# The loads of an attention and feed-forward kernel: Q and K of two batches in 512-byte pieces, V rows loaded once, no transfers issued by ScalarE, small first token blocks

## The chip, the cores and the metric

The kernel runs on one core of a Trainium2 chip. A core has TensorE (PE, with its weight loads listed apart as PEld), VectorE (DVE), ScalarE (ACT), GpSimd (POOL) and SyncE (SP); 16 DMA engines move data between the device's main memory and the core's on-chip memory SBUF. Transfers are issued by SP, ACT or POOL; a row named SPq, ACTq or POOLq in the profile is the time that the issuing queue spent on it. PE writes its results to PSUM, from where ACT or DVE copy them. The metric is the time of one execution on the device, in microseconds.

## The reference

Windowed attention over 8 batches of 8 heads, 576 positions and 64 channels, then a feed-forward layer on the 4,608 tokens.

```python
def _attn_ref(q, k, v):
    ...
    scores = scale * np.matmul(q, k.transpose(0, 1, 3, 2))
    mask = np.abs(pos[:, None] - pos[None, :]) <= window
    scores = np.where(mask, scores, -1000000000.0)
    ...
    attn = attn / (np.sum(attn, axis=-1, keepdims=True) + 1e-09)
    return np.matmul(attn, v)

def _moe_ref(x, w_in, w_out, s, b):
    h = x @ w_in
    r = np.maximum(h, 0.0)
    g = s * (r * r) + b
    return (g @ w_out)
```

The window is 32 positions to each side, the model width 512 (8 heads of 64), the hidden width 2,048. Q, K, V, the weights and the output are float32.

## The kernel before

**Attention.** Each batch is cut into three thirds of 192 positions, each third into two *units* of four heads (two pairs). A unit (`unit`, L420) is a chain: PE scores into the PSUM tile SC (`sc`, L435), ACT exponential (L442), DVE product with the band mask (L445), PE row sums and values (`ss` and `av`, both L458), ACT logarithm and exponential, which give the reciprocal (L465, L468), DVE product into XT (L472). The keys of a third are its 192 positions and 32 on each side, taken as two overlapping blocks of 128. There is one SC, and the scores of a unit wait in PE's order for the `av` of the unit before.

**Getting Q, K and V there.** Per batch, Q and K come in five blocks of up to 128 rows each, V in six blocks of 128 rows, two for each third, that overlap (704 rows in place of 576). A row of one head is 64 float32 numbers, so the pieces of these transfers are 256 bytes (`load`, L289). A block lands in a float32 staging tile (STG, one slot for each block), DVE casts it to bf16 (`cast`, L379), and Q and K are then transposed so that channels lie on partitions: in batch 0 by PE (`transpose_pe`, L402) with a copy out of PSUM by ACT for Q (L407) and by DVE for K (L410); in all later batches by a DMA transpose that SP issues (`transpose_dma`, L387). QT, KT and VB have two slots, for alternate batches; STG and the bf16 tiles NAT have one, so a batch's loads follow the casts of the batch before. Batch 0 is loaded by SP and ACT in turn (`plan0`, L322 to L327), later batches by SP for Q and K and by POOL for V. In batch 1, Q and K wait for the sixth weight piece and V for the seventh.

**Feed-forward.** The tokens are cut into blocks (TBLK, L225): 384, 128, then eight of 512. For each block, stage one (`s1`, `w`, L525) gives 16 tiles of 128 hidden channels with four matmuls each; ACT takes the positive part (L531) and DVE squares it (L534). Stage two (`s2`, `o`, L543) multiplies each 128 tokens with `w_out` in 16 matmuls, DVE scales and adds a constant row (L555), SP stores it (L558). The constant row comes from a column sum of `w_out` (L564, L567). Stage one of a block needs all units whose tokens lie in it. The weights are eight pieces that POOL loads with a cast to bf16 (L310, L314); each waits for the one two before it, the first two for pieces of K and V of batch 0.

**Order.** Every step is a task with an assumed cost, a key and its dependences. `_Graph.plan` (L84) is a planner that takes, again and again, the task that can start first by these costs, the smaller key at a tie; the order is then fixed for each engine, and each engine runs its tasks in that order, waiting on semaphores. The key of a unit is below all stage steps, so a unit goes first once it is ready; `after` holds a unit back until a given step of stage one has started (L505).

## Time and profile before

| | us |
|---|---|
| median of 3 runs (lowest, highest) | 372.65 (370.83, 373.82) |
| the profiled execution | 375.49 |
| its span, first to last instruction | 373.8 |
| PE busy | 319.2 |
| ACT busy | 206.4 |
| DVE busy | 193.2 |
| POOL busy | 44.7 |

The profile shows one execution. The busy time of PE is not PE at its peak, because matmuls are pipelined and their ends are modelled. DMA moved 52.71 MB, of 127,869 packets 116,672 under 512 bytes; 38.80 MB were read from main memory and 9.44 MB written to it. Main readings below are the slices of the span, the table by stretch, the waits, and rows of the timeline in order of time; a bracket at the end of a row tells for how long the engine had been idle and what ended it.

### The profile page before, as it was taken

The numbers are of one execution on the slowest core, as the hardware profiler recorded it, in microseconds if no ns is written. First come the engines' busy times: TensorE is split into PE (matmuls) and PEld (weight loads), VectorE is DVE, ScalarE is ACT, GpSimd is POOL, SyncE is SP. The second block draws the span as 40 slices with busy tenths as digits, with TensorE's granted clock in tenths as the row PEclk, the third lists the DMA queues.
The fourth block names the chain that finished last, engine by engine and source line by source line (L and its number), as shares of the span: only waits on it lengthen the run. The fifth ranks groups of instructions, "written<-read, shape, count | busy, mean of one in ns | idle before, by whom it ended". The sixth has DMA issues, their size and how long they took to land.

```text
span 373.8 us, 6108 instructions
## 1 busy us (share of the span) xinstructions
PE 319.2 (85%) x2385; PEld 155.5 (42%) x2424; DVE 193.2 (52%) x439; ACT 206.4 (55%) x310; POOL 44.7 (12%) x62
## 2 busy tenths in 40 slices
PE   1277985935499999988898899989999999999996
PEld 0144543523244444443444344434444444444442
DVE  4363525745556775676585586454444453333321
ACT  1266732255368678767677576657676764434300
POOL 3012241342221210121111000000000000000000
PEclk9999998975599999999999999999999999999999
DMA  8979999999999999999899798863000001001012
GB/s 164 208 110 187 190 225 206 202 190 213 230 221 147 180 200 231 186 198 193 188 172 213 132 174 174 189 141 89 28 31 31 28 30 56 28 30 56 28 58 84
DMA packets 127869, 52.71 MB, mean 141 GB/s; under 512 B 116672, under 2 KB 120768, under 8 KB 127840
## 3 DMA queue, kind: packets, MB, share of 16 engines
q1 hardware_dynamic: 113648, 36.32, 54.2%
q0 software_dynamic: 7424, 14.29, 19.8%
q10 hardware_dynamic: 6768, 1.70, 2.7%
q8 instruction: 19, 0.31, 0.4%
q14 instruction: 10, 0.08, 0.1%
HBM read 38.80 MB, written 9.44 MB: 129 GB/s over the span
## 4 chain that ended last, share of the span: by engine, by line
PE 54%; DMA 19%; SPq 9%; DVE 7%; ACTq 3%; ACT 3%; issue 2%; DVEq 0%
PE o L543 25%; PE w L525 22%; DMA stgq<-in_q_dram 12%; DMA stgk<-in_k_dram 7%; SPq L300 6%; ACTq L300 3%; SPq L387 3%; PE ss L458 3%; PE sc L435 2%; DVE ex L445 2%; PE av L458 2%; ACT ex L442 1%; DVE xt L472 1%; DVE vb L379 1%; DVE gt L534 1%
## 5 line engine op out<-in xcount | busy, mean ns | idle before, releaser
L525 PE MATMUL w<-xt,win 128*128 128x512 bf16 (+2 forms) x624 | 146.4, 367 | 5.5 <-DVE xt L472 4.2
L543 PE MATMUL o<-wout,gt 128*128 128x512 bf16 x554 | 141.5, 382 | 6.0 <-DVE cvec L567 4.0
L525 PEld LDWEIGHTS w<-xt,win 128*128 128x128 bf16 x640 | 59.4, 100 | 71.8 <-issue 5.1
L543 PEld LDWEIGHTS o<-wout,gt 128*128 128x128 bf16 x576 | 53.2, 98 | 65.5 <-DVE cvec L567 4.2
L442 ACT ACTIVATE ex<-sc,zero 128x1024 bf16<-128x1024 f32 x48 | 53.2, 1109 | 12.1 <-PE sc L435 12.1
L445 DVE TENSOR_TENSOR ex<-ex,mask 128x1024 bf16<-128x1024 bf16 x48 | 33.0, 688 | 33.2 <-ACT ex L442 32.7
L300 POOL DMA_DIRECT2D stgv<-in_v_dram x42 | 35.7, 853 | 120.5 <-DVE vb L379 111.5
L465 ACT ACTIVATE lns<-ss,zero 128x384 f32<-128x384 f32 x48 | 27.7, 578 | 27.6 <-PE ss L458 27.5
L531 ACT ACTIVATE r_29<-w,zero 128x512 bf16<-128x512 f32 (+2 forms) x40 | 25.7, 643 | 30.7 <-PE w L525 30.6
L458 PE MATMUL ss<-ex,ones 128*64 128x128 bf16 x384 | 22.1, 244 | 20.5 <-DVE ex L445 20.1
L531 ACT ACTIVATE r_28<-w,zero 128x512 bf16<-128x512 f32 (+2 forms) x40 | 25.7, 642 | 23.1 <-PE w L525 22.6
L531 ACT ACTIVATE r_31<-w,zero 128x512 bf16<-128x512 f32 (+2 forms) x40 | 25.7, 644 | 23.0 <-PE w L525 22.0
L531 ACT ACTIVATE r_30<-w,zero 128x512 bf16<-128x512 f32 (+2 forms) x40 | 25.7, 643 | 19.2 <-PE w L525 18.8
L555 DVE SCALAR_TENSOR_TENSOR outs<-o,sb_36,cvec 128x512 f32<-128x512 f32 x36 | 26.8, 746 | 13.2 <-PE o L543 12.8
L472 DVE TENSOR_TENSOR xt<-av,rec 128x384 bf16<-128x384 f32 x48 | 26.5, 552 | 11.5 <-ACT rec L468 11.2
L379 DVE CAST natq<-stgq 128x512 bf16<-128x512 f32 (+1 forms) x40 | 17.2, 432 | 25.3 <-DMA stgq<-in_q_dram 25.0
L458 PEld LDWEIGHTS ss<-ex,ones 128*64 128x64 bf16 x384 | 13.6, 119 | 39.6 <-DVE ex L445 26.7
L468 ACT ACTIVATE rec<-lns,zero 128x384 f32<-128x384 f32 x48 | 29.3, 610 | 0.8
L435 PE MATMUL sc<-qt,kt 64*128 64x128 bf16 x384 | 21.2, 237 | 9.0 <-ACT qt L407 5.3
L534 DVE TENSOR_TENSOR gt<-r_29 128x512 bf16<-128x512 bf16 (+2 forms) x40 | 15.8, 396 | 22.7 <-ACT r_29 L531 22.7
L534 DVE TENSOR_TENSOR gt<-r_31 128x512 bf16<-128x512 bf16 (+2 forms) x40 | 15.8, 396 | 22.3 <-ACT r_31 L531 22.0
L534 DVE TENSOR_TENSOR gt<-r_30 128x512 bf16<-128x512 bf16 (+2 forms) x40 | 15.8, 394 | 18.6 <-ACT r_30 L531 18.6
(43 smaller groups left out, 134.4 us busy)
## 6 DMA issues: line engine op xcount, KB each, us to landing
out_dram<-outs SPq DMA_DIRECT2D x36, 256.0 KB, 2.3
stgq<-in_q_dram SPq DMA_DIRECT2D x31, 256.0 KB, 5.8
stgk<-in_k_dram SPq DMA_DIRECT2D x29, 256.0 KB, 6.0
stgv<-in_v_dram POOLq DMA_DIRECT2D x28, 256.0 KB, 5.7
stgv<-in_v_dram POOLq DMA_DIRECT2D x14, 192.0 KB, 5.9
win<-in_moe_w_in_dram POOLq DMA_DIRECT2D x4, 512.0 KB, 6.4
wout<-in_moe_w_out_dram POOLq DMA_DIRECT2D x4, 512.0 KB, 5.8
stgq<-in_q_dram SPq DMA_DIRECT2D x8, 128.0 KB, 5.9
```

Of the source, the lines that this page charges most:

```text
L300: lambda e: e.dma_start(STG[n][p0:p1, blk, :].rearrange("p (h d) -> p h d", h=H), src_of[n][b, :, s0:s0 + ns, :].rearrange("h s d -> s h d ...
L435: fns.append(lambda e, u=u, pr=pr, a=a, hh=hh: e.matmul(SC[:, hh, 256 * u + 128 * a:256 * u + 128 * a + 128], lhsT=KT[slot][64 * hh:64 * h ...
L442: add("act", lambda e: e.activation(EX[e_][:, :, :], SC[:, :, :], AF.Exp, bias=ZERO_F[:, :], scale=0.125), 1130.0, reads=["SC", "ZERO"], w ...
L445: add("dve", lambda e: e.tensor_tensor(EX[e_][:, :, :], EX[e_][:, :, :], MASK[:, :, :], ALU.mult), 700.0, reads=[("E", e_), "MASK"], write ...
L458: fns.append(lambda e, u=u, a=a, hh=hh, dst=dst, lhs=lhs: e.matmul(dst[64 * hh:64 * hh + 64, 192 * u + 64 * a:192 * u + 64 * a + 128], lhs ...
L465: add("act", lambda e: e.activation(LNS[e_][:, :], SS[:, 0:384], AF.Ln, bias=ZERO_F[:, :], scale=1.0), 600.0, reads=["SS", "ZERO"], writes ...
L468: add("act", lambda e: e.activation(REC[e_][:, :], LNS[e_][:, :], AF.Exp, bias=ZERO_F[:, :], scale=-1.0), 600.0, reads=[("LNS", e_), "ZERO ...
L472: add("dve", lambda e: e.tensor_tensor(XT[:, prs[0]:prs[1] + 1, x0:x0 + 192], AV[:, 0:384].rearrange("p (u c) -> p u c", u=2), REC[e_][:, ...
L525: add("pe", [lambda e, kc=kc: e.matmul(W[wb][:, 0:nt], lhsT=WIN_BF[:, kc, ft * 128:(ft + 1) * 128], rhs=XT[:, kc, t0:t0 + nt], start=(kc = ...
L531: add("act", lambda e: e.activation(R1[rb][:, 0:nt], W[wb][:, 0:nt], AF.Relu, bias=ZERO_F[:, :], scale=1.0), 280 + 0.82 * nt, reads=[("W", ...
L534: add("dve", lambda e: e.tensor_tensor(GT[gs][:, ft, 0:nt], R1[rb][:, 0:nt], R1[rb][:, 0:nt], ALU.mult), 160 + 0.53 * nt, reads=[("R1", rb ...
L543: add("pe", [lambda e, fc=fc: e.matmul(O[ob][:, :], lhsT=GT[gs][:, fc, sub * 128:sub * 128 + 128], rhs=WOUT_BF[:, fc, :], start=(fc == 0), ...
```

## The change

Q and K of batches 0 and 1 (`NPE = 2`) are loaded by thirds: `load2` takes two neighbouring rows of a head as one piece of 512 bytes, so a partition holds rows 2p and 2p + 1 of the third, 96 partitions in all. `cast2` casts such a third and puts even and odd rows apart, `transpose_pe` transposes it in eight PE transposes of 96 rows, and one copy, which interleaves even and odd columns again, brings it to QT or KT: in batch 0 by ACT for Q and DVE for K, over the four banks of W and O; in batch 1 by DVE for both, over the two halves of SC. Batches 2 to 7 keep their blocks and the DMA transposes.

V is loaded by POOL in every batch, each row once (pieces of 96, 128, 64, 128, 64, 96 rows); the 64 rows that two blocks share are copied by a second cast, `cast_v`. ACT issues no transfers. The weights no longer wait for anything and stand in POOL's queue behind V of batch 0; Q and K of batch 1 still wait for the sixth piece. The token blocks are 384, 128, 256, 384, six of 512, and 384. In batch 0 the scores of a unit no longer wait for the `av` of the unit before, and units of batches 0 and 1 are held back by nothing else; from batch 2 on, `rel` counts back from the block that needs a unit (PACE, LEAD). The logarithm is written to the tile of the reciprocal. Dependences on QT and KT are kept by 64 columns (`grans`) instead of 128.

```diff
-sizes = [384, 128]
+sizes = [384, 128, 256, 384]
...
-    STG = {n: sb((128, NBLK, DM), F32, "stg" + n) for n in "qk"}
-    STG["v"] = sb((128, 2 * NT3, DM), F32, "stgv")
-    NAT = {n: sb((128, NBLK, DM), BF16, "nat" + n) for n in "qk"}
+    STG = {n: sb((128, 6, DM), F32, "stg" + n) for n in "qkv"}
+    NAT = {n: sb((128, 6, DM), BF16, "nat" + n) for n in "qk"}
...
-    LNS = [sb((128, 384), F32, "lns") for _ in range(2)]
...
+    PACE, LEAD = 2.6, 7
+    NPE = 2
+    EVAC0 = {"q": "act", "k": "dve"}
...
-    def load(b, n, blk, stream="sp", waits=()):
+    VROWS = [(WIN, 128), (0, 128), (64, 128), (0, 128), (64, 128), (0, 96)]
+    def key_of(b, part):
+        return 16 * (b - 1) + part
+    def load(b, n, blk, waits=()):
         if n == "v":
-            k0 = 192 * (blk // 2) - WIN + 128 * (blk % 2)
-            p0, p1 = max(0, -k0), min(128, S - k0)
-            s0 = k0 + p0
+            p0, p1 = VROWS[blk]
...
-            stream,
+            "pool" if n == "v" else "sp",
...
-            1070.0 if stream != "pool" else 1900.0, writes=[("STG", n, blk)],
-            key=16 * (b - 2), waits=waits,
-            dma=({"sp": "l", "act": "a", "pool": "w"}[stream], ns * 9.3))
+            900.0 if n == "v" else 1070.0, writes=[("STG", n, blk)], key=key_of(b, -16), waits=waits,
+            dma=("v" if n == "v" else "l", ns * 9.3))
+    def load2(b, n, t, waits=()):
+        return add(
+            "sp",
+            lambda e: e.dma_start(
+                STG[n][0:96, 2 * t:2 * t + 2, :].rearrange("p a (h x) -> p (a h) x", h=NPAIR),
+                src_of[n][b, :, 192 * t:192 * t + 192, :].rearrange("h (p r) d -> p h (r d)", r=2),
+            ),
+            1000.0, writes=[("STG", n, 2 * t), ("STG", n, 2 * t + 1)], key=key_of(b, -16), waits=waits,
+            dma=("l", 768 * 27 / 16.0))
...
-        return add("pool", fn, 1000.0, writes=[("W" + which, i)], waits=waits, key=-50,
+        return add("pool", fn, 1000.0, writes=[("W" + which, i)], waits=waits, key=-30,
                    dma=("w", 2550.0))
...
-    first = {}
-    plan0 = [("q", 0, "sp"), ("k", 0, "act"), ("q", 1, "sp"), ("k", 1, "act"), ("v", 0, "sp"),
...
-             ("v", 5, "sp")]
-    for n, blk, stream in plan0:
-        first[n, blk] = load(0, n, blk, stream)
+    for n, t in (("q", 0), ("k", 0), ("k", 1), ("q", 1), ("k", 2), ("q", 2)):
+        load2(0, n, t)
+    for blk in range(6):
+        load(0, "v", blk)
...
-    wts = []
-    for i in range(8):
-        wait = [first["k", 3]] if i == 0 else [first["v", 5]] if i == 1 else [wts[i - 2]]
-        wts.append(load_weights("in" if i < 4 else "out", i % 4, waits=wait))
+    wts = [load_weights("in" if i < 4 else "out", i % 4) for i in range(8)]
...
+    def cast_v(b, blk):
+        slot = b % 2
+        key = key_of(b, -8)
+        pad = [("STGPAD", blk)] if blk in (0, 2 * NT3 - 1) else []
+        p0 = 64 if blk in (2, 4) else 0
+        add("dve", lambda e: e.tensor_copy(VB[slot][p0:128, blk, :], STG["v"][p0:128, blk, :]),
+            380.0, reads=[("STG", "v", blk)] + pad, writes=[("VB", slot, blk)], key=key)
+        if blk in (2, 4):
+            add("dve", lambda e: e.tensor_copy(VB[slot][0:64, blk, :], STG["v"][64:128, blk - 1, :]),
+                380.0, reads=[("STG", "v", blk - 1)], writes=[("VB", slot, blk)], key=key,
+                accum=False)
...
-        add("sp", lambda e: e.dma_start(dst[:, :, s0:s0 + ns], NAT[n][0:ns, blk, :],
-                                        transpose=True),
-            1300.0, reads=[("NAT", n, blk)], writes=[(n + "T", slot, blk)],
-            dma=("t", 700.0), key=16 * (b - 1) - 6)
+        c0 = s0 if n == "q" else s0 + WIN
+        add("sp", lambda e: e.dma_start(dst[:, :, c0:c0 + ns], NAT[n][0:ns, blk, :], transpose=True),
+            1250.0, reads=[("NAT", n, blk)], writes=grans(n, slot, s0, s0 + ns),
+            dma=("t", 1000.0), key=key_of(b, -6))
+    def cast2(b, n, t):
+        add("dve", lambda e: e.tensor_copy(
+            NAT[n][0:96, 2 * t:2 * t + 2, :].rearrange("p r (h d) -> p r h d", h=H),
+            STG[n][0:96, 2 * t:2 * t + 2, :].rearrange("p a (g r d) -> p r (a g) d", r=2, d=D)),
+            700.0, reads=[("STG", n, 2 * t), ("STG", n, 2 * t + 1)],
+            writes=[("NAT", n, 2 * t), ("NAT", n, 2 * t + 1)], key=key_of(b, -8))
...
+    def transpose_pe(b, n, t, banks, evac):
+        slot = b % 2
...
-        res = banks[tcount[b] % len(banks)]
-        tcount[b] += 1
...
-        add("pe", [lambda e, pr=pr: e.transpose(view[:, pr, 0:ns],
-                                                NAT[n][0:ns, blk, pr * 128:(pr + 1) * 128],
-                                                IDENT[0:ns, 0:ns]) for pr in range(NPAIR)],
...
+        res, bank = banks[tcount["n"] % len(banks)]
+        tcount["n"] += 1
+        view = bank.bitcast(BF16)[:, 0:768].rearrange("p (r g c) -> p r g c", r=2, g=NPAIR)
+        c0 = 192 * t + (0 if n == "q" else WIN)
+        to = dst[:, :, c0:c0 + 192].rearrange("p g (x r) -> p r g x", r=2)
+        key = key_of(b, -6)
+        add("pe", [lambda e, r=r, pr=pr: e.transpose(view[:, r, pr, :],
+                                                     NAT[n][0:96, 2 * t + r, pr * 128:(pr + 1) * 128],
+                                                     IDENT[0:96, 0:96])
+                   for r in range(2) for pr in range(NPAIR)],
+            450, reads=[("NAT", n, 2 * t), ("NAT", n, 2 * t + 1), "IDENT"], writes=[res], key=key)
+        fn = (lambda e: e.copy(to, view)) if evac == "act" else (lambda e: e.tensor_copy(to, view))
+        add(evac, fn, 900, reads=[res], writes=grans(n, slot, 192 * t, 192 * t + 192), key=key)
...
-        add("pe", fns, 310.0, reads=qk_res, writes=["SC"], key=key + 0.5,
-            after=after + ([("av", n - 1)] if n > 1 else []), name=("qk", n))
+        add("pe", fns, 310.0, reads=qk_res, writes=[("SC", 0), ("SC", 1)], key=key + (0.5 if b > 0 else 0),
+            after=after + ([("av", n - 1)] if b > 0 else []), name=("qk", n))
...
-        add("act", lambda e: e.activation(LNS[e_][:, :], SS[:, 0:384], AF.Ln,
+        add("act", lambda e: e.activation(REC[e_][:, :], SS[:, 0:384], AF.Ln,
                                           bias=ZERO_F[:, :], scale=1.0),
...
+    rel, nxt = {}, 1e9
+    for b in range(B - 1, 0, -1):
+        for t in range(NT3 - 1, -1, -1):
+            for g2 in (1, 0):
+                nxt = min(nxt - PACE, 16 * first_block(b * S + 192 * t) - LEAD)
+                rel[b, t, g2] = nxt
     for b in range(B):
-        if b > 0:
+        banks = ([(("W", 0), W[0][:, :]), (("W", 1), W[1][:, :]), (("O", 0), O[0][:, :]),
+                  (("O", 1), O[1][:, :])] if b == 0 else
+                 [(("SC", hh), SC[:, hh, :]) for hh in range(2)])
+        if b < NPE:
+            steps = [("q", 0), ("k", 0), ("k", 1), 0, ("q", 1), ("k", 2), 1, ("q", 2), 2]
+            if b > 0:
+                for x in steps:
+                    if isinstance(x, tuple):
+                        load2(b, *x, waits=[wts[5]] if b == 1 else ())
+                for blk in range(6):
+                    load(b, "v", blk)
+        else:
+            steps = [0, 1, 2]
             for blk in range(NBLK):
                 for n in "qk":
-                    load(b, n, blk, waits=[wts[5]] if b == 1 else ())
-            for blk in range(2 * NT3):
-                load(b, "v", blk, "pool", waits=[wts[6]] if b == 1 else ())
...
-        for n, blk in order:
-            cast(b, n, blk)
...
+                    load(b, n, blk)
+            for blk in range(6):
+                load(b, "v", blk)
...
+            for blk in range(NBLK):
+                for n in "qk":
+                    cast(b, n, blk)
+                    transpose_dma(b, n, blk)
+        for x in steps:
+            if isinstance(x, tuple):
+                cast2(b, *x)
+                transpose_pe(b, *x, banks, EVAC0[x[0]] if b == 0 else "dve")
                 continue
-            if b == 0:
-                transpose_pe(b, n, blk, banks, "act" if b == 0 and n == "q" else "dve")
-            else:
-                transpose_dma(b, n, blk)
-        for t in range(NT3):
+            cast_v(b, 2 * x)
+            cast_v(b, 2 * x + 1)
...
             for g2 in range(2):
...
-                    i = 3 * (b - 1) + t
-                    r = 32 + 6 * (i - 3) - 7 + 3 * g2
-                    r = max(r, 0 if i < 3 else 32)
-                    after = [("s1", r // 16, r % 16)]
-                unit(b, t, g2, after)
+                r = int(rel[b, x, g2]) if b >= NPE else -1
+                unit(b, x, g2, [("s1", r // 16, r % 16)] if r >= 0 else [])
```

54 lines of the change are left out of this document (13 added, 41 removed).

## The prediction

> **What bounds the kernel now.** I read the page's slices first, then the busy time by stretch, then the waits and the timeline of the stretches that are not full. The slices show busy tenths of 40 slices of 9.3 us: PE, its granted clock, and the share and rate of the DMA engines.
>
> ```profile
> PE   1277985935499999988898899989999999999996
> ...
> PEclk9999998975599999999999999999999999999999
> DMA  8979999999999999999899798863000001001012
> ```
>
> DMA is full to about 235 us, PE is full from 100 us on. The table by stretch (start:end, length, then busy time of PE, PEld, DVE, ACT, POOL, then clock, DMA share, GB/s) is cut at the first stage-one matmul (31.88), the first score matmul of batch 1 (75.2), the next stage-one matmul (99.25) and the last transpose (255.15):
>
> ```profile
> 0.00:31.88 31.88, 12.31 (x144) 8.29 (x144) 14.86 (x42) 13.14 (x19) 6.05 (x16) 1.00 1.01 166
> 31.88:75.20 43.32, 37.83 (x245) 20.12 (x250) 20.79 (x58) 18.01 (x38) 13.85 (x17) 0.96 1.18 201
> 75.20:99.25 24.05, 8.97 (x146) 6.46 (x146) 12.76 (x27) 13.26 (x18) 6.45 (x9) 0.58 1.17 210
> 99.25:255.15 155.90, 145.94 (x1171) 68.34 (x1191) 98.73 (x224) 107.19 (x157) 18.37 (x22) 0.99 1.05 183
> 255.15:373.80 118.65, 114.11 (x683) 52.29 (x695) 46.11 (x90) 54.81 (x80) 0.00 (x0) 0.99 0.11 43
> ```
>
> After 99.25 PE works with few gaps to the end. So the end is set by PE's work, and what can be won are PE's losses, nearly all before 99.25. The waits of PE (engine, line, releaser: us in total, times, longest), the first two from the stretch 31.88 to 99.25, the last two from 100 on:
>
> ```profile
> PE ss L458 <- DVE ex L445: 11.8, 6, 2.0
> PE w L525 <- DVE xt L472: 4.2, 2, 3.3
> ```
>
> ```profile
> PE sc L435 <- DMA kt<-natk: 3.7, 2, 2.0
> PE ss L458 <- DVE ex L445: 3.6, 3, 1.6
> ```
>
> The start (timeline rows: start, length, engine, line):
>
> ```profile
> 4.10 0.29 POOL L353 TENSOR_SCALAR_AFFINE_SELECT mask<-mask 128x128 bf16<-128x128 bf16 x1
> 4.79 0.43 DVE L379 CAST natq<-stgq 128x512 bf16<-128x512 f32 x1 [1.68 <-DMA stgq<-in_q_dram]
> 12.12 2.38 ACTq L300 DMA_DIRECT2D stgk<-in_k_dram  x1
> 14.54 0.59 ACT L407 COPY qt<-w 128x512 bf16<-128x512 bf16 x1 [12.44 <-issue]
> 15.76 0.61 PE L435 MATMUL sc<-qt,kt 64*128 64x128 bf16 x8 [5.35 <-ACT qt L407]
> 16.40 1.11 ACT L442 ACTIVATE ex<-sc,zero 128x1024 bf16<-128x1024 f32 x1 [0.79 <-PE sc L435]
> 17.55 0.69 DVE L445 TENSOR_TENSOR ex<-ex,mask 128x1024 bf16<-128x1024 bf16 x1 [4.64 <-ACT ex L442]
> 18.97 0.58 ACT L465 ACTIVATE lns<-ss,zero 128x384 f32<-128x384 f32 x1 [0.98 <-PE ss L458]
> 20.48 0.42 DVE L410 COPY kt<-w 128x512 bf16<-128x512 bf16 x1 [1.56 <-PE w L402]
> 20.96 0.60 ACT L468 ACTIVATE rec<-lns,zero 128x384 f32<-128x384 f32 x1
> 21.85 0.55 DVE L472 TENSOR_TENSOR xt<-av,rec 128x384 bf16<-128x384 f32 x1
> 30.37 0.61 PE L435 MATMUL sc<-qt,kt 64*128 64x128 bf16 x8
> 31.88 2.74 PE L525 MATMUL w<-xt,win 128*128 128x384 bf16 x8 [0.91 <-DVE xt L472]
> ```
>
> ACT's copies of Q wait behind its own DMA issues until 14.54, although the first data were cast from 4.79 on. Then the units (one third, two head pairs) follow each other every (30.37 - 15.76) / 4 = 3.65 us, since each score group waits for the unit before it. Stage one starts at 31.88.
>
> The hole in the middle, and below it the price of plain PE work (from the chain of waits: start, length, engine, line, count):
>
> ```profile
> 41.98 0.37 SPq L300 DMA_DIRECT2D stgq<-in_q_dram  x1
> 42.24 0.74 POOL L314 DMA_DIRECT2D wout<-in_moe_w_out_dram  x1 [2.26 <-DMA wout<-in_moe_w_out_dram]
> 59.13 0.43 DVE L379 CAST natq<-stgq 128x512 bf16<-128x512 f32 x1 [6.99 <-DMA stgq<-in_q_dram]
> 62.56 1.31 SPq L387 DMA_TRANSPOSE qt<-natq  x1
> 74.93 1.19 SPq L387 DMA_TRANSPOSE kt<-natk  x1
> 75.20 0.40 PE L435 MATMUL sc<-qt,kt 64*128 64x128 bf16 x8
> 77.53 0.41 PE L458 MATMUL ss<-ex,ones 128*64 128x128 bf16 x8 [1.93 <-DVE ex L445]
> 99.25 1.06 PE L525 MATMUL w<-xt,win 128*128 128x512 bf16 x2 [3.27 <-DVE xt L472]
> ```
>
> ```profile
> 316.67 0.86 PE w L525 x4
> ```
>
> Batch 1 is asked for at 41.98, its ten transposes are issued from 62.56 to 74.93, and its six units then run alone, since the third token block (512 wide) needs all of them. A 512-wide matmul costs 0.86 / 4 = 0.215 us; a unit has three groups of about 0.40 us with some overlap, 1.1 us in all. From 31.88 to 99.25 PE did 64 stage-one equivalents (13.8 us), 64 of stage two (13.8), 16 for the column sum (3.4) and 8 units (8.8): 39.8 us in 67.4. **27.6 us are lost there.**
>
> DMA rates, each for its own window: Q and K alone in 256-byte pieces (8 to 15 us), the POOL queue beside SP's (46 to 59, two rows), weights alone (34 to 41), and the output's 2 KB pieces (368 to the end, 40 slices of GB/s):
>
> ```profile
> DMA packets 5884, 1.48 MB, mean 212 GB/s; under 512 B 5884, under 2 KB 5884, under 8 KB 5884
> ```
>
> ```profile
> q0 software_dynamic: 947, 1.94, 71.9%
> q1 hardware_dynamic: 3548, 0.89, 44.8%
> ```
>
> ```profile
> DMA packets 1309, 1.31 MB, mean 187 GB/s; under 512 B 32, under 2 KB 1309, under 8 KB 1309
> ```
>
> ```profile
> GB/s 0 0 99 381 339 395 410 184 0 0 0 0 0 0 0 0 0 0 0 0 0 0 0 0 0 0 141 381 410 339 395 142 0 0 0 0 0 0 0 0
> ```
>
> **The change part by part.** The sum is made against the profiled execution (375.49 us, 0.8% above the median of the runs shown).
>
> *512-byte pieces.* Not in the trace; between 212 GB/s (256 B) and about 390 (2 KB). I take 300, nearer to the 256-byte row's side by the piece's size. A batch's Q and K (2.36 MB) then take 7.9 us, between 6.1 and 11.1. The Trainium skill, page "DMA: Bandwidth & Descriptors", section Specifications, puts the line rate at pieces from 512 B up; by that rule the 390 of the output would hold, and the first stage-one matmul would come about 1 us earlier than I say; the 256-byte row agrees that smaller pieces are slower, 512 no run shows yet.
>
> *A. The start: -8 us.* ACT's issues leave the path. The first third needs three loads of 0.39 MB. The first Q and K pieces (0.52 MB, 2.5 us at 212) were in at 4.79, so data flow from about 2.2 us; at 300 GB/s the three are in at 6.5. A cast of 1,024 elements is two rows of 0.43, 0.9 us (strided reads: up to 1.3); eight transposes 0.6 like a score group; an evacuation of 768 columns 0.6 to 0.9 by the rows of 0.42 and 0.59 for 512. First scores at about 9.5 instead of 15.76. In batch 0 the wait for the unit before is dropped, so the pitch falls to what DVE does for a unit: mask 0.69, product 0.55, and half a third's casts and copies (two wide casts 1.8, two to three V casts 1.1, K's copy 0.7): 3.0 us. Four units: 9.5 + 4.9 (chain of one) + 9 = 23.4. The second third of K comes after V, which POOL now issues from about 4.4 us: if the queues share evenly what the two moved in 46 to 59 (2.83 MB in 13 us, 218 GB/s, so 109 each), the second thirds of Q and K (0.79 MB) are in at 13.7, 3 us of cast, transposes and copy lead to scores at 16.7, and two units end at 24.6. I take stage one at 24 against 31.88. Bounds: 20 (V and weights take little) and 35 (first rival): -12 to +3.
>
> *B. The hole: -20 us.* From 24 PE has stage one of blocks 0 and 1, both their stage twos, the column sum, two units: some 35 us of work, to about 59. Weights follow V without waits: V (1.18 MB) by 15, then eight pieces of 0.52 MB at the 187 of their row, 2.8 us each, the sixth at 32, the last at 37. Batch 1's Q and K are released by the sixth, 10 us earlier than 41.98. Beside the rest of the weights and V of batch 1 (2 MB) the first third is in at about 45, all at 50. The DMA transposes, 12.4 us of issues by the rows 62.56 and 74.93, are gone for this batch; cast, transposes and copy take some 3 us, so units run from 48. The next block (256 tokens) needs only two of them, done at about 56, before PE is out of work at 59. The hole closes but for the slow clock at the start of stage one (2.74 us for 8 matmuls of 384, twice what 0.215 gives) and a few waits: I keep 7 of 27.6. Bounds: 3 and 21 kept (-25 to -7).
>
> *C. Later waits: -3 us.* The two rows after 100 hold 7.3. V falls from 704 to 576 rows a batch (1.44 to 1.18 MB, 1.2 us of DMA at 212), and each later batch needs 4.7 MB with its transposes, some 23 us, plus 3 of output, against 37 us of PE work, so DMA should run ahead. Two more V casts a batch (0.43 each) go to DVE, which was busy 99 of 156 us after 99.25: 0, hidden; without that cover 6 us in all. Bounds -7 to +6.
>
> *D. PE transposes of batch 1: +3 us.* 48 of them, six groups at 0.40 to 0.61: 2.4 to 3.7; while they hold the score banks no unit starts, which counts in B.
>
> *E. Four small blocks: +0.5.* Same columns, 64 more stage-one matmuls and ACT and DVE passes, hidden (ACT was busy 107 of 156 us after 99.25); bounds 0 to 2. LNS written in place: its new wait, for the product two units before, is long past: 0. SP loses no time by it; POOL's V waits for casts as before.
>
> Sum: -8 - 20 - 3 + 3 + 0.5 = -27.5, so 348.0 for the profiled execution, and by 372.65 / 375.49 a median of **345 us**.
>
> **The rivals.**
> *1. POOL crowds out Q and K (356).* V and all weights are now queued by about 16 us, without waits. In the window 46 to 59 SP's pieces got 0.89 of 2.83 MB, 31%, beside POOL's. If packets take equal turns, 512 B against 1.94 MB / 947 = 2,050 B, SP gets 20% of 218 GB/s, 44 GB/s, and the second third (0.79 MB after 6.5 us) comes at 24.5. With 3 us to the scores, a chain of 4.9 and a pitch of 3.0 stage one starts at 35: 11 us more in A, 356. For it: batch 1's second Q came at 59. Against: 31%, not 11%, for 256-byte pieces. The Trainium skill, same page, section "Queues, rings and completion order", has each engine go round its queues a packet at a time; the shares of this window lie between equal turns and equal bytes.
>
> *2. The hole moves to batch 2 (355).* Batch 2 still comes in 256-byte pieces with ten DMA transposes. Batch 1 took 33 us from 41.98 to 75.2; from 50 that is 83, and six units at 3.65 end at 105. PE runs dry at about 104 (24, plus 77 us of work of blocks 0 to 3 summed under the next rival, plus some waits), so this is at the edge; SP runs in order, and if batch 2's loads or transposes stand 10 us behind outputs that wait for stage two, PE waits those 10. For it: 1.17 DMA share at that time. Against: V and Q, K are lighter and the units of batch 2 can start while blocks 2 and 3 run.
>
> *3. The other side: the clock (385).* In 75.2 to 99.25 the clock was 0.58 with waits of 1.93 us between short groups. The new start strings transposes, units and narrow blocks together in just that way. Blocks 0 to 3 hold 1,152 tokens: 62 us of the two stages, 3.4 of column sum, 9 of units, 3 of transposes, 77 in all. At 0.58 all of it costs 56 us more; from 31 us more (the clock low over somewhat more than half) the kernel is slower than before; 385 with 40. Against: 0.96 in 31.88 to 75.2, with the same mix. The Trainium skill, page "TensorE: Matmul & The Clock Gate", Part 1, lets the clock fall after an idle window of about 3.4 us; the waits of 1.9 us that went with 0.58 are shorter, so here the trace is harsher than the rule.
>
> *4. No change (372).* Should the sixth weight land as late as now, batch 1 is not earlier, and the start's gain is waited away in front of it. Against: the POOL waits between weights are gone.
>
> **How the numbers follow.** Forecast 0.59, first rival 0.18, second 0.14, third 0.06, fourth 0.03. Faster by over 1% (what a measurement of this kernel can tell from no change): 0.59 + 0.18 + 0.14 = 0.91, less 0.01 for mixed cases: 0.90; within 1% 0.04; slower 0.06. The range takes the forecast's lower bounds in A and B together with some of C (332) and reaches over the first two rivals with a few us of B's upper bound (362).
>
> **What would show it.** A: ACT has no DMA rows, first scores near 9.5, pitch near 3, stage one at 22 to 26; a K cast waiting for DMA past 18 us speaks for the first rival. B: batch 1's scores from about 48, no transposes on SP before those of batch 2, clock 0.9 or more from 30 us on. C: no wait of scores on DMA over 2 us after 100; a PE wait of 8 us or more around 100 speaks for the second rival. D: six groups of eight transposes at 0.4 to 0.6. I am wrong if the clock stays near 0.5 between 30 and 95, or if PE has a hole there although the data are in.

## The result and the profile after

| | before | after |
|---|---|---|
| median, first measurement (us) | 373.24 (370.83 to 377.25) | 357.00 (354.79 to 360.06) |
| median, second measurement (us) | 375.84 (373.38 to 379.68) | 356.72 (356.67 to 358.15) |
| profiled execution (us) | 375.49 | 354.85 |
| its span (us) | 373.8 | 353.1 |

The ratio was 0.959 with an interval of 0.947 to 0.972, and 0.953 (0.947 to 0.959) when the changed kernel was measured again beside some of the experiments. Faster, as forecast, and 357 lies in the range of 332 to 362, but 12 us above the 345 that was predicted. The ratios of the experiments below are to be held against these two. The profiles of runs 3, 4 and 9 are of executions that were 1 to 2% longer than the fastest of those kernels, so only differences far above that are read from them.

The slices of the changed kernel (40 slices of 8.8 us, busy tenths): PE's 3, 5 and 4 of the ninth to eleventh slice, with a clock of 7, 5 and 5 there, are gone.

```profile
PE   1256999699976999999999999999999999999995
PEclk9999999999999899999999999999999999999999
DMA  7999999996998999999899997630000000010102
```

The table by stretch of the changed kernel (start:end, length, busy time of PE, PEld, DVE, ACT, POOL, clock, DMA share, GB/s), cut at its first stage-one matmul, at batch 1's first scores and at 120 us:

```profile
0.00:35.37 35.37, 14.27 (x185) 10.25 (x185) 19.28 (x40) 16.28 (x21) 19.28 (x32) 1.00 1.08 199
35.37:61.60 26.23, 26.05 (x167) 13.79 (x169) 16.42 (x35) 11.52 (x22) 5.46 (x6) 1.00 1.16 208
61.60:120.00 58.40, 49.87 (x520) 28.81 (x528) 45.77 (x118) 41.03 (x74) 12.12 (x15) 0.97 1.01 181
120.00:353.10 233.10, 226.60 (x1636) 108.34 (x1664) 127.47 (x274) 138.58 (x208) 12.56 (x15) 1.00 0.55 113
```

Two things are to be seen. Stage one starts **later** than before, at 35.37 instead of 31.88. From there on PE hardly waits: it is full until batch 1's units begin, and in the 58 us after that the clock stays at 0.97, where the stretch of the lone units had 0.58 before. Its waits in the stretch 35.37 to 100 (engine, line, releaser: total, times, longest):

```profile
PE o L577 <- DVE outs L589: 2.6, 1, 2.6
PE ss L480 <- DVE ex L467: 2.0, 2, 1.8
PE w L559 <- ACT r_27 L565: 0.2, 1, 0.2
```

Before, the stretch 31.88 to 99.25 had 11.8 and 4.2 us in its two longest groups alone.

The start of the changed kernel (timeline: start, length, engine, line; the bracket tells the idle time before and what ended it):

```profile
5.21 0.89 DVE L414 CAST natq<-stgq 96x1024 bf16<-96x1024 f32 x1 [2.10 <-DMA stgq<-in_q_dram]
7.30 1.01 DVE L414 CAST natk<-stgk 96x1024 bf16<-96x1024 f32 x1 [1.21 <-DMA stgk<-in_k_dram]
9.16 0.71 DVE L414 CAST natk<-stgk 96x1024 bf16<-96x1024 f32 x1 [0.55 <-DMA stgk<-in_k_dram]
...
13.28 0.61 PE L457 MATMUL sc<-qt,kt 64*128 64x128 bf16 x8 [0.65 <-DVE kt L436]
13.92 1.11 ACT L464 ACTIVATE ex<-sc,zero 128x1024 bf16<-128x1024 f32 x1 [0.24 <-PE sc L457]
18.59 0.69 DVE L414 CAST natk<-stgk 96x1024 bf16<-96x1024 f32 x1 [5.37 <-DMA stgk<-in_k_dram]
...
20.09 0.61 PE L457 MATMUL sc<-qt,kt 64*128 64x128 bf16 x8
...
21.11 0.67 DVE L467 TENSOR_TENSOR ex<-ex,mask 128x1024 bf16<-128x1024 bf16 x1
...
23.78 0.69 DVE L414 CAST natq<-stgq 96x1024 bf16<-96x1024 f32 x1 [1.55 <-DMA stgq<-in_q_dram]
```

The first scores come at 13.28, not at the 9.5 predicted. The first exponential ends at 15.0, but its mask product starts only at 21.11: DVE runs in order, and ahead of the mask stood the cast of K's last third, which waited 5.37 us for its data. PE in turn had that third's transposes ahead of the second unit's scores. Q's second third had long been in (cast at 11.08). Q's last third, which the first token block doesn't need, is cast at 23.78, again ahead of a mask: the second unit's, which starts at 24.39, though its exponential had ended at 21.85.

The transfers of 9.5 to 18.5 us in the changed kernel (all packets; then each queue's packets, MB, share of its time; q0 is POOL's, q1 SP's):

```profile
DMA packets 1735, 1.89 MB, mean 210 GB/s; under 512 B 118, under 2 KB 1466, under 8 KB 1735
q0 software_dynamic: 548, 1.29, 71.6%
q1 hardware_dynamic: 1187, 0.60, 39.5%
```

SP's pieces got 0.60 of 1.89 MB, 32%. And batch 1 (timeline, SP and PE): its loads are issued from 35.42, one of them is stuck for 10.62 us, and its first scores come at 61.60.

```profile
35.78 1.12 SPq L320 DMA_DIRECT2D stgk<-in_k_dram  x2
36.95 10.62 SPq L320 DMA_DIRECT2D stgq<-in_q_dram  x1
...
61.60 0.40 PE L457 MATMUL sc<-qt,kt 64*128 64x128 bf16 x8
```

### The profile page after: what moved, and what is told of

It reads as the page before. It is cut to its first block, busy times and chain, and to the rows that moved or that the text cites. A ratio compares the mean times of both kernels' runs of the same rounds, so it can differ in the third digit from the quotient of the medians.

```text
span 353.1 us, 6377 instructions
## 1 busy us (share of the span) xinstructions
PE 316.8 (90%) x2502; PEld 161.2 (46%) x2544; DVE 208.9 (59%) x467; ACT 207.4 (59%) x324; POOL 49.4 (14%) x68
## 3 DMA queue, kind: packets, MB, share of 16 engines
q0 software_dynamic: 7360, 13.64, 19.9%
## 4 chain that ended last, share of the span: by engine, by line
PE 74%; DMA 12%; SPq 5%; DVE 4%; ACT 3%; issue 2%
PE o L577 32%; PE w L559 32%; DMA stgq<-in_q_dram 9%; PE ss L480 4%; SPq L309 4%; PE sc L457 3%; PE av L480 3%; DMA stgk<-in_k_dram 3%; SPq L320 1%; ACT ex L464 1%; DVE ex L467 1%; DVE vb L390 1%; DVE gt L568 1%; ACT rec L487 1%; DVE xt L494 1%
## 5 line engine op out<-in xcount | busy, mean ns | idle before, releaser
L559 PE MATMUL w<-xt,win 128*128 128x512 bf16 (+3 forms) x690 | 149.6, 346 | 2.6 <-ACT r_28 L565 0.9
L577 PE MATMUL o<-wout,gt 128*128 128x512 bf16 x548 | 140.0, 380 | 4.7 <-DVE outs L589 2.6
L559 PEld LDWEIGHTS w<-xt,win 128*128 128x128 bf16 x704 | 64.0, 99 | 66.2 <-issue 3.2
L464 ACT ACTIVATE ex<-sc,zero 128x1024 bf16<-128x1024 f32 x48 | 53.3, 1110 | 11.5 <-PE sc L457 11.4
L309 POOL DMA_DIRECT2D stgv<-in_v_dram x48 | 39.8, 833 | 139.6 <-DVE vb L390 104.3
L565 ACT ACTIVATE r_26<-w,zero 128x512 bf16<-128x512 f32 (+3 forms) x44 | 26.8, 608 | 28.9 <-PE w L559 28.2
L565 ACT ACTIVATE r_29<-w,zero 128x512 bf16<-128x512 f32 (+3 forms) x44 | 26.8, 608 | 21.5 <-PE w L559 21.1
L565 ACT ACTIVATE r_27<-w,zero 128x512 bf16<-128x512 f32 (+3 forms) x44 | 26.8, 609 | 21.0 <-PE w L559 20.5
L565 ACT ACTIVATE r_28<-w,zero 128x512 bf16<-128x512 f32 (+3 forms) x44 | 26.8, 608 | 20.2 <-PE w L559 20.2
L487 ACT ACTIVATE rec<-ss,zero 128x384 f32<-128x384 f32 x48 | 27.7, 576 | 17.2 <-PE ss L480 17.1
L589 DVE SCALAR_TENSOR_TENSOR outs<-o,sb_34,cvec 128x512 f32<-128x512 f32 x36 | 26.9, 748 | 13.7 <-PE o L577 13.7
L490 ACT ACTIVATE rec<-rec,zero 128x384 f32<-128x384 f32 x48 | 29.4, 612 | 0.7
L568 DVE TENSOR_TENSOR gt<-r_29 128x512 bf16<-128x512 bf16 (+3 forms) x44 | 16.4, 373 | 21.3 <-ACT r_29 L565 21.0
L568 DVE TENSOR_TENSOR gt<-r_28 128x512 bf16<-128x512 bf16 (+3 forms) x44 | 16.4, 373 | 20.3 <-ACT r_28 L565 20.2
L568 DVE TENSOR_TENSOR gt<-r_27 128x512 bf16<-128x512 bf16 (+3 forms) x44 | 16.4, 374 | 19.4 <-ACT r_27 L565 19.1
L480 PE MATMUL ss<-ex,ones 128*64 128x128 bf16 x384 | 21.2, 236 | 7.2 <-DVE ex L467 5.6
L568 DVE TENSOR_TENSOR gt<-r_26 128x512 bf16<-128x512 bf16 (+3 forms) x44 | 16.4, 373 | 13.9 <-ACT r_26 L565 13.8
L390 DVE CAST vb<-stgv 128x512 bf16<-128x512 f32 (+1 forms) x48 | 21.0, 443 | 4.9 <-PE av L480 4.1
```

The source lines that it names most:

```text
L309: lambda e: e.dma_start(STG[n][p0:p1, blk, :].rearrange("p (h d) -> p h d", h=H), src_of[n][b, :, s0:s0 + ns, :].rearrange("h s d -> s h d ...
L464: add("act", lambda e: e.activation(EX[e_][:, :, :], SC[:, :, :], AF.Exp, bias=ZERO_F[:, :], scale=0.125), 1130.0, reads=[("SC", 0), ("SC" ...
L480: fns.append(lambda e, u=u, a=a, hh=hh, dst=dst, lhs=lhs: e.matmul(dst[64 * hh:64 * hh + 64, 192 * u + 64 * a:192 * u + 64 * a + 128], lhs ...
L487: add("act", lambda e: e.activation(REC[e_][:, :], SS[:, 0:384], AF.Ln, bias=ZERO_F[:, :], scale=1.0), 600.0, reads=["SS", "ZERO"], writes ...
L490: add("act", lambda e: e.activation(REC[e_][:, :], REC[e_][:, :], AF.Exp, bias=ZERO_F[:, :], scale=-1.0), 600.0, reads=[("REC", e_), "ZERO ...
L559: add("pe", [lambda e, kc=kc: e.matmul(W[wb][:, 0:nt], lhsT=WIN_BF[:, kc, ft * 128:(ft + 1) * 128], rhs=XT[:, kc, t0:t0 + nt], start=(kc = ...
```

## The experiments

Each starts from the changed kernel, unless it says otherwise. All ratios are to the kernel before, measured beside it; the runs were measured in four groups (1 to 4; 5, 6, 7 and 9; 8, 10 and 11; 12), so between groups the ratios are compared and not the medians.

| what is different | median, us | ratio (95% interval) |
|---|---|---|
| weights behind batch 0's Q and K | 363.18 | 0.967 (0.963 to 0.970) |
| batch 1 as before | 359.71 | 0.957 (0.952 to 0.963) |
| 256-byte pieces | 367.76 | 0.978 (0.973 to 0.983) |
| old blocks | 359.88 | 0.959 (0.953 to 0.965) |
| masks before K's last third | 351.13 | 0.937 (0.931 to 0.943) |
| batch 1 and blocks as before | 364.36 | 0.972 (0.967 to 0.977) |
| the same and the old release | 364.37 | 0.970 (0.963 to 0.976) |
| V rows twice | 355.55 | 0.941 (0.931 to 0.950) |
| masks first, V held back | 355.11 | 0.946 (0.938 to 0.953) |
| masks first, first block 192 | 358.65 | 0.954 (0.947 to 0.961) |
| all but the start as before | 370.89 | 0.988 (0.983 to 0.993) |

**1. Do the weights crowd out batch 0's Q and K?** The first weight piece waits for batch 0's last load of Q; the order of the work stays.

```diff
+        wts[0].deps.add(lastqk)
```

> Only the first weight piece is given a wait, for the last Q piece of batch 0 (the other seven stand behind it in POOL's queue); the order of all engines is that of the changed kernel. Theory (weights and V on POOL's queue crowd the second and third thirds of Q and K, whose casts stand in DVE's order ahead of the first units' masks): the cast of K's last third comes at 14 to 16 instead of 18.6, that of Q's at 18 to 20 instead of 23.8, stage one starts at 29 to 32 instead of 35.4, and the time falls by 4 to 6 us to about 351 (0.945 of the kernel before). Rival (the start is set by the copies and the order, not by the transfers): stage one stays within 1 us of 35.4 and the time within 2 us. Other side: the weights land some 4 us later, so that the column sum (now at 47.9) or batch 1, which waits for the sixth piece, gives it back: stage one earlier, time the same.

The cast of K's last third came at 19.54 (18.59 with the weights queued freely), the first stage-one matmul at 36.37 (35.37). Four other runs with the start of the changed kernel (2, 4, 5 and 7) have 19.92 to 21.17 and 36.94 to 38.14, so these differences are no larger than those between executions: nothing came earlier, and the weights are not what holds up K's last third. Of POOL's transfers that leaves V, which run 10 tries. But the weights came later, batch 1's scores started at 68.25 and not at 61.60 (PE waited 5.7 us for its K), and the total was 363.2 us. What the early queueing of the weights buys lies behind the start.

**2. Batch 1 as before**, in 256-byte pieces with DMA transposes. By the same constant its units are then also released by `rel`.

```diff
-        NPE = 2
+        NPE = 1
```

> Batch 1 goes back to 256-byte blocks and DMA transposes (and waits for the sixth weight piece as before); all else as changed. Theory (the hole before 99 us came from batch 1's slow way in): batch 1's scores start at 72 or later instead of 61.6, PE has a hole of 10 us or more between 60 and 90, and the time rises by 8 to 15 us to 365 to 372. Rival (the small blocks and the freed order alone close the hole): at most 3 us more than the changed kernel.

Batch 1's scores came at 71.72, ten us later than in the changed kernel, and the total did not move: 0.957, inside what the changed kernel itself gave. The 10 us are waited for in one place (13.64 us of PE work between 60 and 80) and not in the other (19.63 and 19.41 us between 80 and 120).

**3. The size of the pieces alone.** The same thirds, each as two transfers with 256-byte pieces.

```diff
+                [lambda e, r=r: e.dma_start(
+                    STG[n][0:96, 2 * t + r, :].rearrange("p (h d) -> p h d", h=H),
+                    src_of[n][b, :, 192 * t:192 * t + 192, :].rearrange("h (p r) d -> r p h d", r=2)[r],
+                ) for r in range(2)],
```

> The thirds of batches 0 and 1 are loaded in 256-byte pieces (two transfers for each third, even and odd rows), everything else and all orders as changed. The rate of 512-byte pieces seen in the changed kernel between 5.5 and 9.5 us was 217 GB/s in all, hardly over the 212 of 256-byte ones. Theory one (pieces of 512 bytes are worth a third more rate, as predicted): K's first third is cast 2 us later, stage one starts 4 us or more later, and the time rises by 4 to 8 us. Theory two (the rate of the loads is set by something else than the piece, by now): casts within 1 us, time within 2 us of the changed kernel.

Stage one started at 52.50 and the total rose to 367.8 us: 15 to 17 us later at the start cost some 7 to 9 in the end. Transfers of 9.5 to 18.5 us in this run:

```profile
q0 software_dynamic: 653, 1.13, 72.2%
q1 hardware_dynamic: 2080, 0.52, 48.9%
```

Beside POOL's transfers SP's queue got 0.52 of 1.66 MB, 31%, almost the share that it has with pieces twice as large; but the whole ran at 184 GB/s and not at 210, and V flowed sooner (0.36 MB of POOL's between 7 and 9.5 us, against 0.08). By 9.5 us SP's queue had moved 1.08 MB, in the changed kernel 1.54. What was not in by then had to come at SP's share, 0.06 to 0.07 MB a us in both: K's last third was cast at 30.84, Q's at 40.92. The run also doubles the number of transfers, and SP issued those of K's last third only from 7.80 to 14.45 us, so it doesn't separate the size of the pieces from their being queued later.

**4. The old token blocks** (384, 128, then 512).

```diff
-    sizes = [384, 128, 256, 384]
+    sizes = [384, 128]
```

> Token blocks 384, 128, then 512 as before; all else as changed. Theory (the third block of 512 needs all six units of batch 1, that of 256 only two): after block 1 PE waits for the units of batch 1, whose last ends near 90 us: a hole of 6 to 12 us between 70 and 95 and 5 to 10 us more time, 362 to 367. Rival (with batch 1 early enough the block size does not matter): within 2 us of the changed kernel, or 1 to 2 us better, for fewer narrow matmuls.

0.959: no difference that shows beside 0.959 and 0.953. PE loses time in another place: 28.5 us of PE work in the 40 us from 80 to 120, where the changed kernel has 34.4 (32.8 in run 5).

**5. The changed kernel once more.**

> The changed kernel once more, as the measure for the runs beside it: 0.959 of the kernel before, between 0.950 and 0.968, and a first stage-one matmul within 1 us of 35.4 us, PE short waits around 100 to 120 us.

0.953; stage one at 37.48, 2 us later than in the first profile and outside the microsecond that I had allowed, the first mask again behind K's last third (20.45 and 22.97). Another wait of the same kind is longer here: at 103.08 PE had waited 5.93 us for a mask of batch 2. Its exponential had ended at 95.90, but DVE stood at a cast of batch 3 whose data were not in.

```profile
100.44 0.43 DVE L402 CAST natq<-stgq 128x512 bf16<-128x512 f32 x1 [6.46 <-DMA stgq<-in_q_dram]
...
102.33 0.69 DVE L467 TENSOR_TENSOR ex<-ex,mask 128x1024 bf16<-128x1024 bf16 x1
```

**6. The order at the start.** The planner assumes that a third of 0.39 MB takes 1.3 us. For batch 0 this guess is multiplied by 2.6; nothing else is touched, and so the masks of the first units stand ahead of the cast of K's last third.

```diff
-                dma=("l", 768 * 27 / 16.0))
+                dma=("l", (2.6 if b == 0 else 1.0) * 768 * 27 / 16.0))
```

> Only the planner's guess of how long a load of batch 0 takes is raised (times 2.6), so that VectorE has the masks of the first units ahead of the cast of K's last third and TensorE their scores ahead of its transposes. Theory 'order': the late start of stage one (35.4 us) is the order written for a faster DMA; the first mask comes at 15 to 17 us instead of 21.1, stage one starts at 28 to 32 us, and the total falls by 3 to 6 us (ratio to before about 0.947). Rival 'supply': stage one starts as early, but the PE then waits later, between 40 and 120 us, for data that come no sooner; the total moves by less than 2 us (0.955 to 0.963). Rival 'data': the first masks do move, yet stage one stays at 34 us or later, since the last third of Q and K (23.8 us) is what it waits for.

Its timeline:

```profile
14.63 0.69 DVE L467 TENSOR_TENSOR ex<-ex,mask 128x1024 bf16<-128x1024 bf16 x1 [1.29 <-ACT ex L464]
...
19.53 0.69 DVE L414 CAST natk<-stgk 96x1024 bf16<-96x1024 f32 x1 [2.33 <-DMA stgk<-in_k_dram]
...
34.88 2.74 PE L559 MATMUL w<-xt,win 128*128 128x384 bf16 x8
```

The mask moved by 6.5 us, stage one by only 0.5 (from 35.37) to 2.6 us (from 37.48 in run 5), the total by 5.6 us, to 351.1: the best version found, ahead of both kernels. The total is what theory "order" asked for, but stage one stands near 35 us, as the rival "data" says, and at least half of the gain lies later. Between 80 and 120 us PE was busy for 36.4 us, where run 5 has 32.8: the same edit shifts the whole plan, and which part of that comes from the masks isn't separated.

**7. Are batch 1's way and the small blocks covers for the same hole?** Runs 2 and 4 in one kernel.

> Batch 1 the old way (256-byte pieces, DMA transposes, released by the sixth weight) and the old token blocks (384, 128, then 512) together; each of them alone cost nothing that could be measured. Theory 'substitutes': each alone covers the hole, together they bring it back: batch 1's scores at 68 to 72 us with the third block waiting for all six units, a PE hole of 8 us or more between 60 and 100 us, the total 8 to 17 us above the changed kernel (ratio to before 0.98 to 1.005). Rival 'lighter traffic': the hole was closed by less traffic and by weights without waits; the total stays within 3 us of the changed kernel (0.95 to 0.967).

The hole is back, 364.4 us, 7.6 above the changed kernel of the same measurement. Its table by stretch (80 to 100 us) and its waits from 60 to 110 us:

```profile
80.00:100.00 20.00, 10.02 (x100) 5.73 (x99) 12.17 (x27) 9.93 (x14) 4.84 (x6) 0.50 1.19 224
```

```profile
PE ss L480 <- DVE ex L467: 12.1, 6, 2.4
```

Six units alone, a clock of 0.50, waits of up to 2.4 us: the picture of the kernel before. Each of the two parts alone keeps it away; neither shows a gain on top of the other. Yet the run still stands 11 us below the kernel before, which the next runs look for.

**8. The old rule for releasing units**, on top of run 7.

```diff
-                    r = int(rel[b, x, g2]) if b >= NPE else -1
+                    i = 3 * (b - 1) + x
+                    r = max(32 + 6 * (i - 3) - 7 + 3 * g2, 0 if i < 3 else 32) if b else -1
```

> Batch 1 and the token blocks as before (the run that stood at 0.972 of the kernel before) and also the rule by which the units of later batches are released against stage one as before. What still separates that run from the kernel before is some 11 us, of which the waits of TensorE after 130 us (9.1 us before, 0.4 us there) are the larger part. Theory 'release rule': the old rule brings those waits back, 6 to 9 us between 130 and 240 us, ratio 0.985 to 1.0. Rival 'lighter DMA load': the waits on kt from the transposes and on the masks do not come back, since V's rows are fewer and batch 0 and the weights are out of the way earlier; ratio 0.967 to 0.977.

0.970 against 0.972: the rule is worth nothing here, and the waits after 130 us did not come back (0.4 us).

**9. V rows twice**, on the changed kernel.

```diff
-        VROWS = [(WIN, 128), (0, 128), (64, 128), (0, 128), (64, 128), (0, 96)]
+        VROWS = [(WIN, 128), (0, 128), (0, 128), (0, 128), (0, 128), (0, 96)]
```

> V as before (overlapping rows loaded twice, 704 rows a batch instead of 576, one cast a block and not two for the blocks with shared rows). If the first 115 us are bound by what the DMA engines deliver (some 210 GB/s), the 0.26 MB more for each of the first three batches come to 3.7 us: the total rises by 2 to 5 us (ratio 0.965 to 0.973). Rival: the two extra casts of VectorE a batch weigh as much or more, and the total stays or falls (0.950 to 0.960).

0.941, interval 0.931 to 0.950, beside 0.953 (0.947 to 0.959): loading V's rows once has no gain that shows on the changed kernel, though stage one began at 40.34 in this run, the latest but that of run 3. The second casts go with the extra rows, and DVE was busy for 200.0 us instead of 209.7.

**10. V held back** until K's second third has landed, on top of run 6. The planner is told that V and the weights are ready from 6 us on, and so may order some later steps differently.

```diff
+        for x in v0:
+            x.ready = 6000.0
...
+        for x in wts:
+            x.ready = 6000.0
...
+        v0[0].deps.add(k1)
```

> As the run with the masks ahead of K's last third, and V of batch 0 is asked for only when K's second third has landed (some 8 us instead of 3.6 us; the weights stay behind V). In the changed kernel the pieces of 512 bytes flowed at 338 to 380 GB/s between 3 and 4 us and at 110 to 190 GB/s between 5 and 8 us, while nothing but them was moved and POOL was issuing V. Theory 'POOL issuing slows SP's queue': 5 to 8 us runs at 250 GB/s or more, K's second third is cast at 7 to 8 us and not at 10.2, first scores at 10 to 11 us instead of 12.8; V's first block lands at 12 to 14 us. Rival 'the dip has another cause' (the kernel before has one too, 148 GB/s between 5 and 6 us, with POOL idle): the rate stays under 200 GB/s and the first scores stay at 12 to 13.5 us. In both cases the weights land 4 to 5 us later (first stage-one matmul 35 to 39 us), so the total is 351 to 357 us by this chip's measure (ratio to before 0.937 to 0.953).

The rate from 6 to 8 us was 224 and 213 GB/s (146 in run 6, but 222 and 240 in the first profile of the changed kernel, with POOL issuing V), between 5 and 6 it was 133, the cast of K's second third stayed at 10.2 and the first scores at 12.88: holding V back doesn't bring the first three loads in earlier. But K's last third was cast at 15.29 and not at 19.53, Q's at 18.07 and not at 24.99, and stage one began at 31.90: the share that V takes does hold the last thirds up. The weights came later in turn, batch 1's scores started at 64.69 after PE had waited 6.6 us for its K, PE had 13.83 us of work between 60 and 80, and the ratio was 0.946 against 0.937 in run 6, with intervals that overlap: 3 us earlier at the start brought nothing in the end. Here the queue of SP was alone from 9 to 12 us:

```profile
DMA packets 1236, 0.62 MB, mean 207 GB/s; under 512 B 26, under 2 KB 1236, under 8 KB 1236
q1 hardware_dynamic: 1236, 0.62, 115.4%
```

Pieces of 512 bytes, nothing beside them, all engines busy: 207 GB/s, and 216 from 2.2 to 12 us. The 256-byte pieces of the kernel before had 212.

**11. A first token block of 192**, on top of run 6. Stage two runs over whole groups of 128 tokens, so the last 64 tokens of both blocks of 192 are left out of it: 16 matmuls of 512, some 3.4 us.

```diff
-    sizes = [384, 128, 256, 384]
+    sizes = [192, 192, 128, 256, 384]
```

> As the run with the masks ahead of K's last third, and the first token block of 384 is split into 192 and 192, so that stage one needs two units and the first piece of the weights (it landed at 22.7 us there). Theory 'stage one waits for four units': stage one starts at 25 to 28 us instead of 34.9, TensorE is busier by 4 to 6 us between 25 and 36 us, and the total falls by 2 to 5 us (ratio to before 0.924 to 0.933). Rival 'supply': stage one starts early but then waits for the later weight pieces (the last of the first four landed at 31.5 us) and for batch 1, with 192-column matmuls that cost more per token (0.10 to 0.12 us each, against 0.08 by columns); total within 2 us or up to 4 us longer (0.933 to 0.948).

Stage one began at 34.44, as with 384, since its first matmul stands in PE's order behind the scores of three later units (25.58, 28.45, 31.16), which waited for the last thirds (K's cast at 22.91, Q's at 28.31); and the total was 358.7 us (0.954 against 0.937 in run 6), longer in spite of the work left out. PE had 11.54 us of work between 20 and 40, run 6 had 14.72. The theory has no support.

**12. All but batch 0's own start as before**: runs 7 and 8, V rows twice, and the weights chained as before.

```diff
+            wait = [k2] if i == 0 else [v5] if i == 1 else [wts[i - 2]]
+            wts.append(load_weights("in" if i < 4 else "out", i % 4, waits=wait))
...
+                    load(b, "v", blk, waits=[wts[6]] if b == 1 else ())
```

> Everything but batch 0's own start as before: batch 1 and blocks, release rule, V's rows twice, and the weights chained (the first behind K's last third, the second behind V's last block, each other one behind the weight two ahead; batch 1's V behind the seventh). Theory 'account closed by supply': the 11 us that the run with batch 1, blocks and release rule as before still stood below the kernel before came from the queue of the weights and from V's rows; they come back, with first scores of batch 1 at 76 to 82 us, less data moved by 75.2 us (under 14.3 MB, against 14.7 there and 14.0 before), and the ratio to before is 0.99 to 1.02. Rival 'the start': the gain lies in batch 0 itself (no issues on ACT, thirds, no chain between units), the ratio stays at 0.965 to 0.98, though stage one starts no earlier than 34 us.

0.988, against 0.970 in run 8: the chain of the weights and V's rows together bring back about 7 of the 11 us, between what the theory (0.99 or more) and the rival (0.98 or less) had asked for. Batch 1's scores came at 76.84. The waits of POOL's queue in this run show where the time in the chain goes:

```profile
POOL win L329 <- DMA stgk<-in_k_dram: 10.8, 1, 10.8
POOL win L329 <- DMA win<-in_moe_w_in_dram: 6.4, 2, 4.2
POOL wout L333 <- DMA win<-in_moe_w_in_dram: 4.4, 2, 2.5
POOL wout L333 <- DMA wout<-in_moe_w_out_dram: 4.2, 2, 2.3
```

And the first 75.2 us in the tables by stretch, of the kernel before, of this run, and of the changed kernel:

```profile
0.00:75.20 75.20, 50.13 (x389) 28.41 (x394) 35.65 (x100) 31.16 (x56) 19.90 (x33) 0.98 1.11 186
```

```profile
0.00:75.20 75.20, 49.59 (x395) 28.52 (x396) 36.78 (x95) 31.54 (x54) 25.71 (x39) 0.98 1.02 181
```

```profile
0.00:75.20 75.20, 51.20 (x491) 30.89 (x496) 46.94 (x105) 36.16 (x60) 26.26 (x40) 1.00 1.12 203
```

186 and 181 GB/s with the chain, 203 without it: over 75.2 us that is 1.3 MB more than before, or some 6 us of transfers at 207 GB/s. Run 8, which differs from run 12 by the chain and V's rows alone, has 195 GB/s, 1.1 MB more than run 12. How much of the 7 us is the chain's and how much that of the rows, no run separates.

## Why the prediction was right, and where it was not

The forecast, faster mainly by the closing of the hole, was right. By its own sum the profiled execution should have lost 27.5 us, and lost 20.6. That it comes this close owes something to luck, for two misses offset each other: the start by 11.5 us, and what lies behind it by 4.7 the other way.

**A, the start, failed: +3.5 us (35.37 against 31.88) instead of -8.** Two of its steps were wrong. The first is the rate of 300 GB/s for 512-byte pieces, "nearer to the 256-byte row's side", which was still too high: alone and with the engines full they ran at 207 (run 10, 9 to 12 us; 216 from 2.2 to 12), no faster than the 212 that I had named as the lower bound. The row to trust was the 256-byte one. The Trainium skill, page "DMA: Bandwidth & Descriptors", section Specifications, puts the line rate at pieces from 512 bytes up; run 10 does not agree, since 207 GB/s is far from the 390 of the output's stores. The second step is "if the queues share evenly": SP's queue got 32% beside POOL's. The loads come in the order of need, so what the second third of the units lacked was not Q's second third (cast at 11.08) but K's last: it was cast at 18.59, where I had these data in at 13.7. What I had not priced at all is what stands behind the late cast in an engine's order: the first unit's mask, ready at 15.0, ran at 21.11. Run 6 moved this mask by 6.5 us and stage one's start by 0.5 to 2.6, run 10 with less of V beside it by another 3. With both undone it stood at 31.90, still 8 us behind the forecast; the 3.54 MB of batch 0's Q, K and V alone take 17 us at 207 GB/s, from 2.2 us on. That is the **first rival's** mechanism: V crowds out the data of the second third, and stage one at its 35 us. The 31% from the stretch 46 to 59 was the right number, which I set aside; the weights, which the rival names beside V, are cleared by run 1. The total ended near its 356 as well, but that is partly chance: the rival kept my B and C, and neither came out as written. Nor does a shift of the start reach the end as I added it up: 3 us earlier brought nothing (run 10), 15 to 17 later cost 7 to 9 (run 3).

**B, the hole, came out smaller than forecast, and its cause was right only in part.** By idle time alone PE lost 8.7 us from 35.37 to 120 (0.2 before batch 1's scores, 8.5 after), where it had been idle for 20.6 from 31.88 to 99.25. The 27.6 that I started from count the slow clock too. Counted in that way, by the same prices and with the transposes as work, PE did about 72 us of work in the 84.6 (132 matmuls of 512 columns' worth of stage one, 112 of stage two, 16 for the column sum, nearly twelve units): an estimate of 13 us lost, where I kept 7. And batch 1's scores came at 61.60 and not at 48: the loads of batch 1 went out at 35.4 (I had the sixth weight at 32) and then ran beside POOL's transfers: 0.68 of the 2.28 MB moved from 36.9 to 47.6 us were SP's. So the hole was not closed because batch 1 was early. Run 2 had its scores at 71.72 and the same total. It was closed because PE had other work meanwhile: either the small blocks, which need only some of the units, or batch 1 by thirds, of which either is enough (runs 2, 4 and 7). I had named both and added them up as if both were needed.

**C, later waits, was right in sign and too small.** The two groups that I had quoted at 7.3 us lay behind 130 us, and the changed kernel has no wait of either kind there. What its profile has after 100 us is one wait, at 114, which belongs to the second rival:

```profile
PE ss L480 <- DVE ex L467: 2.2, 1, 2.2
```

I predicted -3. By the estimate above, PE lost 15 us from 99.25 to the end before, and 4 from 120 to the end in the changed kernel, so some 11 were won here. My reason, lighter transfers of V, has no support: V rows twice (run 9) did not bring the waits back (0.9 us after 130), nor did the old release rule (run 8), nor the chain of the weights (run 12, no wait of PE after 130 us). All three runs share the changed planner costs, batch 0's new start and the finer dependences on QT and KT, and which of these matters is open; none of the runs undid them.

**D and E, the transposes and the blocks, cost nothing that shows.** Eight transposes took 0.82 us in batch 0 (I had 0.6) and 0.51 to 0.52 in batch 1, and copies of 768 columns 0.99 to 1.02 (0.6 to 0.9). Runs 2 and 4, each without one of the two, are no faster. From the first stage-one matmul to the end the profiled executions took 341.9 and 317.7 us, 24.2 less; B, C, D and E together were to give 19.5. So what the sum has wrong is A by 11.5, and the rest by 4.7 the other way.

**The second rival**, a hole at batch 2, is there in part: the longest wait of PE between 100 and 120 is 2.24 us, and 5.93 when the kernel was profiled again (run 5); the 8 that would have decided for it are not reached. DVE's order stands behind both:

```profile
108.98 0.43 DVE L402 CAST natk<-stgk 128x512 bf16<-128x512 f32 x1 [1.18 <-DMA stgk<-in_k_dram]
111.65 0.43 DVE L402 CAST natq<-stgq 128x512 bf16<-128x512 f32 x1 [2.24 <-DMA stgq<-in_q_dram]
...
113.27 0.68 DVE L467 TENSOR_TENSOR ex<-ex,mask 128x1024 bf16<-128x1024 bf16 x1
```

Casts of batch 3 stand ahead of a mask of batch 2 and wait for their data. **The third**, the clock, did not come: 0.97 between 61.60 and 120 (0.94 in run 5), where work of stages one and two lies between the short groups; in run 7, where the units run alone, it is 0.50. **The fourth**, no change, fell with the sixth weight: its wait for the ones before was gone, and run 12 shows what this chain costs.

Where the 18 us of the second measurement went, by the ratios (0.953 is 18 us below 1): undone step by step, batch 1's way or the small blocks are worth about 7 us (run 7), the release rule 0 (run 8), the chain of the weights with V's rows about 7 (run 12; on the changed kernel, run 9, the rows alone show nothing), and 4 to 5 us remain that belong to what no run undid: batch 0's start, the planner's costs, the finer dependences. In this last part the later start of stage one (36.16 in run 12) is a loss, so the gain must lie behind it; what makes it isn't shown. Undone in another order, the parts need not have the same worth.

## What to carry to other kernels

When a fixed order is written from guessed transfer times, a guess that is too short adds its own harm to a late transfer: ready work stands behind the step that waits, as the masks did here at 21.11 and 102.33 us. A longer guess for the first loads, with nothing else touched, was worth 5.6 us, though which part of that is the masks' isn't separated. Two parts of a change that each fill the same hole must not be added up; undo them singly and together before either gets the credit. And price a transfer size by the nearest row that was measured with the queues full, not by a peak: what moved with the time here was how steadily the queues were fed (203 against 186 GB/s over 75 us) and who shared them.
